# One kernel, two heads: exponential tables from integer phases and real magnitudes, and a new division of PSUM

## The chip, the cores and the metric

The kernel runs on one core of a Trainium2 chip. The metric is the device time of one execution in microseconds (us). The core has a matrix engine (TensorE, PE in the profile), a vector engine (VectorE, DVE), an activation engine (ScalarE, ACT), GpSimd (POOL) and SyncE (SP), whose queue issues nearly all of the transfers between HBM and the on-chip memory (SBUF). Matrix products land in PSUM, which has eight banks of 128 partitions x 512 words of four bytes.

## What is computed

Two heads of 512 columns each, for 2048 rows, are put side by side.

```
a = x @ dft_hid_re.T ; b = x @ dft_hid_im.T          # head A (FNet): x is 2048 x 512
yA = dft_seq_re @ a - dft_seq_im @ b                 # 2048 x 2048 matrices, given as inputs

dt = exp(log_dt)                                     # head B (S4D): 512 channels, 128 states
A  = -exp(log_A_real) + 1j * A_imag
C  = (C_real + 1j * C_imag) * dt[:, None]
P  = exp((A * dt[:, None])[:, :, None] * arange(2048))
K  = 2 * einsum("dn,dnl->dl", C, P).real             # a kernel of 2048 taps for each channel
yB = irfft(rfft(u, 4096) * rfft(K, 4096))[:2048] + u * D_skip
```

## The kernel before

**One order for all engines.** Nothing on the chip decides the order of the work. A planner in the program (class `Plan`) runs while the kernel is built: each step is a Python generator that yields the engine it wants and a duration that the planner books (`act(n)`, `dve(n)`, `load(kb)` or a constant for PE), and the step that can start first, by urgency among equals, is emitted next. Each engine then works through its list in that order and waits where an operand isn't there. Buffers and permits are `Sem` and `Ring` objects, completed values `Event` objects. An operation that takes longer on the chip than the planner booked does not change the order; it delays what stands behind it.

**Head A, class `Fnet`.** Four rows of a sequence matrix S that belong together (n, 1024 + n, 1024 - n, 2048 - n) agree up to their sign when S is a true DFT matrix. So of each four rows one (`base`) is multiplied in fp32 with the folded x, and the other three enter only by their deviations from it (`rest`, in bf16). `load_quad` loads one base tile and three `slots` tiles (128x512 fp32 each), computes the three deviations on DVE (L406, `same`, 52 instructions; L411, `own`, nine), writes a bf16 copy of the base (`rough`, L436, on ACT) and squares the deviations on ACT with a running sum (L439) for the guard. There are 32 such quads: four output blocks t, cosine and sine (c), four row blocks k. `sums` multiplies them with the folded x on PE: one fp32 product with the base (L493) and three bf16 products with the deviations (L496) for two column parts of 128, and for the cosine a third part of one column; then four bf16 products with `rough` for each half (L505). `outputs` multiplies the results with the hidden matrix (L558 in fp32, L559 in bf16), `evacuate` stores them. `loads` paces the quads: a group of four is let in every `GROUP_US` = 51 us, a quad every `QUAD_US` = 9 us. `guard` compares the sums of squares with thresholds; if S were not as assumed, `general` would recompute head A after the rest, under a branch.

**Head B, class `Ssm`.** The 2048 taps are split as l = 32 m + n: for each chunk of 32 channels (16 chunks) there are two complex tables, `t1` (32 entries for each channel, with C and dt in it) and `t2` (80 columns before), and PE multiplies them over the 128 states (`taps`, L1045, 64 products of 32 x 80). Both tables are built by repeated doubling. `seed_args` takes the parameters of the chunk, doubles the exponents up to 2^10 on ACT (L897), reduces the phases on DVE (L899 to L903) and takes Exp, Sin and Cos on ACT (L907 to L913); `seeds` multiplies them to complex seeds (L922). `tables1` and `tables2` then double the tables with complex products: `mul` (L852) makes four real products, `add` (L861) sums them. Even entries of `t2` are squares of earlier ones: ACT squares (L868), DVE subtracts (L881) and takes the doubled product (L875). The upper part of `t2` is in two forms, for which L1006 multiplies once more. `taps` is followed by the transform of the kernel along one axis (`stage1_k`, L1071), stored to HBM (`xk`, L1086). Meanwhile `spectrum_u` transforms u (L1125, evacuated by L1132, stored to `xu`). `spectra` reloads both in another order (L1180), `products` and `product` finish the transforms (L1208), multiply spectra (L1225, L1227) and start the inverse (L1241), stored to `zs` (L1253), reloaded (L1275) and finished by `inverse` (L1281, L1294, stored by L1288). The channels go through this in five units of 128, 128, 128, 64 and 64; a unit can start when its last chunk's tables are done.

**PSUM** is divided into four pairs of banks (`f0` to `f3`, permits `fs`), taken by `bank` and by `banks(2)`, which takes two pairs at once. The sums of head A hold one pair (sine) or two (cosine) for a whole group of four quads; `taps`, `stage1_k`, `stage1_u`, `product` and `inverse` take the others.

The last lines of the table step, which both the steps below and the prediction follow:

```
for j in range(4):
    p = yield from self.mul("prod", t, slice(0, 2 ** j), cs[:, :, 6 + j])
    yield from self.add(p, t, slice(2 ** j, 2 * 2 ** j))
```

## Time and profile before

| | |
|---|---|
| median of 2 runs | 529.36 us (529.35 to 529.37) |
| span of the profiled execution, first to last instruction | 527.8 us |
| what lies around the span (median less span; the execution's own time isn't listed apart) | 1.6 us |
| PE busy | 411.4 us, 78% of the span |
| DVE busy | 432.4 us, 82% |
| ACT busy | 362.1 us, 69% |
| moved by DMA | 113.59 MB, 215 GB/s on average |
| mean granted TensorE clock | 0.879 of full speed |

The profile is a page with the busy time of each engine, the span in 40 slices, the chain of work that ended last, and the costliest groups of instructions by line; the trace behind it can be asked for stretches of time, for single shapes and for a timeline. Durations are those of one execution. Matrix products are pipelined, so a busy PE need not be at its peak; where the granted clock is under 1, the same products take longer.

### The profile page before, as it was taken

What the parts mean: (1) busy time and instruction counts of PE and PEld (TensorE: products, weight loads), DVE (VectorE), ACT (ScalarE), POOL (GpSimd) and SP (SyncE); (2) the same over time, 40 slices, a digit from 0 to 9 for tenths busy, and PEclk for the clock granted to TensorE, in tenths of its full rate; (3) what the DMA queues carried; (4) which work ended last, traced back from release to release, by engine and by line L of the source; (5) the groups of instructions that cost most, each with busy time, mean ns of one, the idle gap of its engine ahead of it and who ended that gap; (6) DMA issues with size and microseconds to landing.
All of it is one profiled execution on the core that took longest, in us unless ns stands there. A gap on an engine that the chain in (4) does not pass through costs nothing.

```text
span 527.8 us, 13802 instructions
## 1 busy us (share of the span) xinstructions
PE 411.4 (78%) x5561; PEld 213.2 (40%) x5602; DVE 432.4 (82%) x763; ACT 362.1 (69%) x723; POOL 11.2 (2%) x21
## 2 busy tenths in 40 slices
PE   4589594559997988896999989967994999957421
PEld 3133121335453534353534444534541654646321
DVE  3999599998999899999999999999799999420300
ACT  1559699899699796759798979796587654433210
POOL 0000000000010000000010000003000000000000
PEclk7769886769999899999899999997796899975776
DMA  8989787866159937959959775719494156679851
GB/s 316 315 313 326 262 316 251 280 233 178 44 186 257 309 103 228 275 181 316 309 161 282 214 218 169 221 42 315 124 289 123 42 179 165 167 201 280 216 160 44
DMA packets 142532, 113.59 MB, mean 215 GB/s; under 512 B 68096, under 2 KB 112512, under 8 KB 142208
## 3 DMA queue, kind: packets, MB, share of 16 engines
q1 hardware_dynamic: 141744, 111.47, 68.6%
q10 hardware_dynamic: 720, 1.18, 0.6%
q8 instruction: 46, 0.75, 0.6%
q14 instruction: 22, 0.18, 0.1%
HBM read 78.09 MB, written 34.54 MB: 213 GB/s over the span
## 4 chain that ended last, share of the span: by engine, by line
DVE 36%; PE 30%; DMA 16%; ACT 6%; issue 5%; SPq 3%; POOL 1%; ACTq 0%; DVEq 0%; POOLq 0%
DVE prod L852 10%; PE f L558 6%; DVE t L861 6%; DMA slots<-in_sT 5%; PE f L1045 4%; DVE rest L406 4%; PE f L493 4%; PE f L1241 4%; PE f L1071 3%; DVE t L1006 3%; PE f L1281 3%; PE f L1208 2%; PE f L496 2%; DMA t<-zs 2%; DVE mid L1225 2%
## 5 line engine op out<-in xcount | busy, mean ns | idle before, releaser
L852 DVE TENSOR_TENSOR prod<-t,cs 128x1024 f32<-128x1024 f32 (+4 forms) x160 | 125.3, 797 | 1.9 <-ACT t L987 0.5
L861 DVE TENSOR_TENSOR t<-prod 128x512 f32<-128x512 f32 (+4 forms) x160 | 73.5, 475 | 0.9
L558 PE MATMUL f<-p,w 128*128 128x512 f32 x128 | 68.1, 614 | 6.0 <-ACT y L583 5.5
L406 DVE TENSOR_TENSOR rest<-slots,base 128x512 bf16<-128x512 f32 (+2 forms) x52 | 53.7, 1033 | 6.8 <-DMA slots<-in_sT 5.1
L1045 PE MATMUL f<-t,t 128*32 128x80 f32 x2048 | 45.1, 249 | 14.7 <-ACT big L1132 7.4
L439 ACT ACTIVATE slots<-rest 128x1536 f32<-128x1536 bf16 x32 | 47.3, 1479 | 12.3 <-DVE rest L406 8.6
L493 PE MATMUL f<-base,ec 128*128 128x512 f32 (+1 forms) x96 | 53.4, 639 | 0.0
L1045 PEld LDWEIGHTS f<-t,t 128*32 128x32 f32 x2048 | 40.9, 119 | 25.1 <-ACT big L1132 10.5
L493 PE MATMUL f<-base,es 128*128 128x512 f32 x64 | 38.2, 682 | 10.9 <-ACT xi L266 6.4
L496 PE MATMUL f<-rest,xr 128*128 128x512 bf16 (+1 forms) x134 | 38.8, 390 | 9.1 <-DVE rest L406 8.5
L868 ACT ACTIVATE square<-t 128x256 f32<-128x256 f32 (+1 forms) x64 | 36.3, 568 | 9.8 <-DVE t L881 5.8
L1006 DVE TENSOR_TENSOR t<-t,cs 128x1024 f32<-128x1024 f32 x32 | 38.9, 1217 | 0.0
L558 PEld LDWEIGHTS f<-p,w 128*128 128x128 f32 x128 | 22.5, 191 | 29.9 <-issue 18.6
L1208 PE MATMUL f<-big,w 64*32 64x256 f32 (+1 forms) x1024 | 30.4, 369 | 3.2 <-issue 2.6
L496 PEld LDWEIGHTS <-xr 128*128 128x128 bf16 (+1 forms) x144 | 13.7, 95 | 46.5 <-issue 40.9
L496 PE MATMUL f<-rest,xi 128*128 128x512 bf16 x86 | 27.3, 413 | 6.6 <-DVE rest L406 4.1
L1125 PE MATMUL f<-big,ib 64*128 64x512 f32 x64 | 20.8, 756 | 14.0 <-ACT big L1132 13.2
L1222 ACT ACTIVATE big<-f 128x1024 f32<-128x1024 f32 x28 | 27.4, 1019 | 5.0 <-PE f L1208 5.0
L881 DVE TENSOR_TENSOR t<-square 128x128 f32<-128x128 f32 (+1 forms) x64 | 24.7, 386 | 7.2 <-ACT square L868 7.2
L1071 PE MATMUL f<-ks,f1k 32*128 32x512 f32 (+1 forms) x192 | 22.0, 591 | 3.8 <-POOL ks L1060 3.6
L927 ACT ACTIVATE cs<-cs 128x352 f32<-128x352 f32 x32 | 15.6, 529 | 12.6 <-DVE cs L922 12.5
L1208 PEld LDWEIGHTS f<-big,w 64*32 64x32 f32 x1024 | 18.1, 108 | 14.0 <-issue 6.7
(147 smaller groups left out, 678.6 us busy)
## 6 DMA issues: line engine op xcount, KB each, us to landing
slots<-in_sT SPq DMA_DIRECT2D x93, 256.0 KB, 4.8
xu<-big SPq DMA_DIRECT2D x16, 512.0 KB, 4.5
base<-in_sT SPq DMA_DIRECT2D x31, 256.0 KB, 4.6
xk<-big SPq DMA_DIRECT2D x28, 256.0 KB, 3.4
big<-xu SPq DMA_DIRECT2D x24, 256.0 KB, 5.1
big<-xk SPq DMA_DIRECT2D x24, 256.0 KB, 5.6
zs<-mid SPq DMA_DIRECT2D x24, 256.0 KB, 2.8
big<-zs SPq DMA_DIRECT2D x12, 512.0 KB, 6.0
```

The costliest lines, as they stand in the source:

```text
L406: return v.tensor_tensor(rest[:, lo:hi:step], raw[:, lo:hi:step], base[:, None, :].to_broadcast([128, n, DM]), op=op)
L439: nc.scalar.activation(raw, rest, AF.Square, accum_out=self.stat[:, n:n + 1])
L493: nc.tensor.matmul(out, x[:, cols], base, start=k == 0, stop=False)
L496: nc.tensor.matmul(out, still[:, cols], rest[:, h], start=False, stop=k == 3 and h == 2)
L558: nc.tensor.matmul(ps, self.w[k][:, cols], self.p[t, c][:, d], start=k == 0, stop=False)
L852: self.nc.vector.tensor_tensor(p.rearrange("p k d c m -> p k (d c) m"), src.rearrange("p d c l -> p (d c) l")[:, None, :, rows].to_broadca ...
L861: self.nc.vector.tensor_tensor(dst[:, :, :, rows], p[:, 0], p[:, 1, :, ::-1], op=OP.add)
L868: self.nc.scalar.activation(sq, t[:, :, :, m // 2:m], AF.Square)
L1006: self.nc.vector.tensor_tensor(t[:, :, ::1 - 2 * k, 48 + 16 * k:64 + 16 * k], t[:, :, :, 1:32:2], cs[:, k, 5, :, :, None].to_broadcast([12 ...
L1045: nc.tensor.matmul(ps[32 * j:32 * j + 32, i], t1[:, d, c], t2[:, d, c], start=c == 0, stop=c == 1, tile_position=(0, 32 * j))
L1071: nc.tensor.matmul(out[:, :, 1] if a == 2 else out, self.f1k[r, min(a, 1)], taps, start=a == 0, stop=a == 2, tile_position=(32 * j, 0))
L1208: nc.tensor.matmul(both[:, :, c], self.w2[rows, R * q + r, xx, 32 * c:32 * c + 32], xs[rows, r, xx], start=True, stop=True, tile_position= ...
```

## The change

**Tables.** The complex doubling goes. For each chunk, two tables of phases (`phases1`, `phases2`) are grown by adding integers (a full turn is 2^32, wrapping), and two tables of real magnitudes (`magnitudes1`, `magnitudes2`) by real products; each has 5 or 6 DVE instructions. ACT turns each phase table into real and imaginary parts (`sines`: Abs, Sin, Sin), reading the phases across their layout, and one DVE product per table scales them by the magnitudes. `t2` has 64 columns instead of 80, of which 40 come this way and 24 are squares of earlier ones (`evens`, `squares`). Seeds are made for 64 channels at a time (`SET`), in eight sets; they hold exponents and phases instead of complex values. C enters as a magnitude and an angle, for which `params` computes a reciprocal, an Arctan and two sines, once for the first 64 channels and once for the other 448.

**Head A.** The bf16 copy `rough` goes: the low products read the upper halves of the fp32 base words (every second bf16). So the bases are held until the low products are done; there are 5 instead of 3. `same` becomes an instruction that also keeps the maximum of the deviations; ACT squares only the nine deviations of `own`. In exchange three products for each quad with a stationary column of ones sum the deviations over the partitions, and ACT squares that row once for each of the eight sums. `guard` has 14 small DVE instructions instead of eight.

**PSUM.** Three pairs, one bank `third` (the one-column part and the row of sums; one permit) and one bank `taps`. `stage1_k`, `stage1_u` and the first part of `products` take one pair at a time instead of two; the evacuations become steps of their own.

**Pace and constants.** `GROUP_US` 51 to 30, `QUAD_US` 9 to 6; urgencies of the table steps are new. The 32 inner positions of u are put in another order (`ORDER`) by the host's layout, as is one constant table.

```diff
-            return v.tensor_tensor(rest[:, lo:hi:step], raw[:, lo:hi:step],
-                                   base[:, None, :].to_broadcast([128, n, DM]), op=op)
+            col, self.tops = self.tops, self.tops + 1
+            return v.tensor_tensor_reduce(rest[:, lo:hi:step], raw[:, lo:hi:step],
+                                          base[:, None, :].to_broadcast([128, n, DM]), 1.0, 0.0, op, OP.max,
+                                          self.stat[:, col:col + 1])
...
-        nc.scalar.activation(rough, base, AF.Copy)
...
-        nc.scalar.activation(raw, rest, AF.Square, accum_out=self.stat[:, n:n + 1])
+        for h, n, col in squares:
+            yield "act", act(512 * n) + 0.1
+            nc.scalar.activation(raw[:, h:h + n], rest[:, h:h + n], AF.Square, accum_out=self.stat[:, col:col + 1])
...
+            yield "pe", 0.2 if not c else 0.66, None, 6
+            for h in range(3):
+                nc.tensor.matmul(third[32:33], self.ones, rest[:, h], start=k == 0 and h == 0, stop=k == 3 and h == 2,
+                                 tile_position=(0, 32))
+            self.plan.put(self.rests)
...
-                nc.tensor.matmul(low[:, d], self.xb[t, c, k][:, 128 * d:128 * d + 128], self.m[t, c, k][2], start=k == 0,
-                                 stop=k == 3)
+                nc.tensor.matmul(low[:, d], self.xb[t, c, k][:, 128 * d:128 * d + 128],
+                                 self.m[t, c, k][0].bitcast(BF16)[:, 1::2], start=k == 0, stop=k == 3)
...
-        self.slots, self.fs, self.one = [0, 1, 2, 3], Sem(4), Sem(1)
+        self.slots, self.fs, self.one, self.tapss = [0, 1, 2], Sem(3), Sem(1), Sem(1)
...
+    rises = (5, 4, 1, 1), (6, 4, 2, 2), (8, 4, 4, 3), (12, 4, 8, 4), (3, 1, 1, 4), (20, 0, 20, 5)
...
+    def grow(self, p, seed, to, of, m):
...
+        yield "dve", dve(m * CHUNK)
+        self.nc.vector.tensor_tensor(p[:, to:to + m], p[:, of:of + m],
+                                     seed[:, None, :].to_broadcast([128, m, CHUNK]), op=OP.add)
...
+            for j in range(5):
+                yield from self.grow(p, s[:, 6 + j], 2 ** j, 0, 2 ** j)
...
+    def sines(self, re, im, p, sign):
...
+        a, n = self.nc.scalar, math.prod(re.shape[1:])
+        yield "act", act(n) + 0.15
+        a.activation(re, p, AF.Abs)
+        yield "act", act(n) + 0.15
+        a.activation(im, p, AF.Sin, scale=sign * TWO_PI / TURN)
+        yield "act", act(n) + 0.15
+        a.activation(re, re, AF.Sin, scale=-TWO_PI / TURN, bias=self.halfpi)
...
+    def sines2(self, n):
+        yield self.t2s
+        t, p = self.t2[n % 2], self.p2.rearrange("p (h l) d -> p d h l", h=2)
+        yield from self.sines(t[:, :, :, 0, :20], t[:, :, :, 1, :20], p, 1.0)
...
+        yield from self.sines(t[:, :, 0], t[:, :, 1], self.p1.rearrange("p m d -> p d m"), -1.0)
...
+    def scale(self, p, seed, to, of, m):
...
+        yield "dve", dve(m * CHUNK)
+        self.nc.vector.tensor_tensor(p[:, :, to:to + m], p[:, :, of:of + m],
+                                     seed[:, :, None].to_broadcast([128, CHUNK, m]), op=OP.mult)
...
+            yield "dve", dve(80 * CHUNK)
+            v.tensor_tensor(t, t, p.rearrange("p d (h l) -> p (d h) l", h=2)[:, :, None, :].to_broadcast(
+                [128, 2 * CHUNK, 2, 20]), op=OP.mult)
...
+            yield "dve", dve(64 * CHUNK)
+            v.tensor_tensor(t, t, p[:, :, None, :].to_broadcast([128, CHUNK, 2, 32]), op=OP.mult)
...
+        yield from self.squares(t[:, :, 0, :, 4:20], t[:, :, :, :, 20:28])
+        yield from self.squares(t[:, :, 0, :, 20:28], t[:, :, :, :, 28:])
...
-BASES, SLOTS, RESTS, STAGED, ROUNDS = 3, 2, 2, 2, 6
-GROUP_US, QUAD_US, AHEAD_US = 51.0, 9.0, 20.0
+BASES, SLOTS, RESTS, STAGED = 5, 2, 2, 2
+GROUP_US, QUAD_US, AHEAD_US = 30.0, 6.0, 20.0
```

More of the change, by code (lines that the diff above doesn't have):

```diff
@@ new lines, in load_tables @@
+        self.p1, self.p2 = (tab.tile([128, m, CHUNK], I32, name=f"phase{m}") for m in (32, 40))
+        self.square = tab.tile([128, 16 * CHUNK], F32, name="square")
+        self.mag = tab.tile([128, 72 * CHUNK], F32, name="mag")
+        self.both = [tab.tile([128, 2, 12, SET], F32, name=f"seeds{m}") for m in range(2)]
+        self.par = tab.tile([128, 4, SET], F32, name="par")
+        second = self.t2[1].rearrange("p d h c l -> p (d h c l)")
+        n = DM - SET
+        self.rest = second[:, :4 * n].rearrange("p (a d) -> p a d", a=4)
@@ L818, in setup_rest @@
         yield self.dt_ev
-        yield from self.params(par, par[:, 0], dt)
-        self.plan.put(self.t1s)
-        yield self.pars
-        self.par[1] = self.tab.tile([128, 4, CHUNK], F32, name="par", bufs=2)
-        yield "act", act(4 * CHUNK)
-        self.nc.scalar.activation(self.par[1], par[:, :, :CHUNK], AF.Copy)
-        self.plan.set(self.par1_ev)
+        yield from self.params(par, par[:, 0], dt, self.angle_tmp2)
+        for _ in range(2):
+            self.plan.put(self.t1s)
         yield "dma", load(900)
```

693 lines of the change are left out of this document (373 added, 320 removed).

## The prediction

> **What bounds the kernel now.** I read the page first: the busy times and the slices of the span.
>
> ```profile
> span 527.8 us, 13802 instructions
> PE 411.4 (78%) x5561; PEld 213.2 (40%) x5602; DVE 432.4 (82%) x763; ACT 362.1 (69%) x723; POOL 11.2 (2%) x21
> ...
> DVE  3999599998999899999999999999799999420300
> ```
>
> DVE is nearly full from the second slice to the 34th, then almost idle. So I cut the span where DVE's last table operation ends, at 449 us by the timeline below, and asked for busy time by stretch (columns: length, busy time and count of PE, its weight loads, DVE, ACT and POOL; then the granted TensorE clock, the DMA share and GB/s).
>
> ```profile
> core 0: us, PE busy (x) PEld busy (x) DVE busy (x) ACT busy (x) POOL busy (x), PEclk, DMA share, GB/s
> 20.00:100.00 80.00, 55.80 (x241) 19.66 (x246) 72.72 (x139) 61.92 (x130) 0.00 (x0) 0.77 0.85 298
> 100.00:450.00 350.00, 304.00 (x4123) 154.48 (x4154) 335.10 (x588) 272.54 (x543) 10.16 (x7) 0.94 0.65 198
> 450.00:528.00 78.00, 41.44 (x1177) 33.31 (x1176) 13.03 (x20) 20.57 (x32) 0.23 (x1) 0.75 0.69 181
> ```
>
> From 20 to 450 us, the main stretch, DVE works 72.7 + 335.1 = 407.8 of 430 us, 95%; PE 359.8 (84%) and ACT 334.5 (78%). The last 78 us are another kernel: DVE has 13 us of work, and the last unit of channels goes through its chain of small steps. The timeline and the chain of waits show the seam and one loss in the tail:
>
> ```profile
> 448.63 0.69 DVE L861 TENSOR_TENSOR t<-prod 128x512 f32<-128x512 f32 x1
> 450.07 2.42 PE L1045 MATMUL f<-t,t 128*32 128x80 f32 x128
> 460.09 2.06 ACT L1078 ACTIVATE t<-f 128x512 f32<-128x512 f32 x4 [1.33 <-PE f L1071]
> 470.15 2.37 SPq L1086 DMA_DIRECT2D xk<-t  x4
> ```
>
> The last taps start 0.8 us after DVE's last table operation: the end is set by when the tables are done, plus a tail. In the tail the last store of `xk` had its data at 462.15 us and was issued at 470.15, behind other transfers in SP's queue. The span is 1.6 us short of the median of 529.36; I add that back at the end.
>
> **DVE, the tables.** What goes is nine groups, L852 to L903 (below L852, L861 and the last; L1006, L881, L875, L922, L899 and L901 lie between):
>
> ```profile
> L852 DVE TENSOR_TENSOR prod<-t,cs 128x1024 f32<-128x1024 f32 (+4 forms) x160 | 125.3, 797 | 1.9 <-ACT t L987 0.5
> L861 DVE TENSOR_TENSOR t<-prod 128x512 f32<-128x512 f32 (+4 forms) x160 | 73.5, 475 | 0.9
> L903 DVE TENSOR_SCALAR seed<-seed 128x352 f32<-128x352 f32 x16 | 5.3, 334 | 0.0
> ```
>
> Their sum is 317.9 us. For what comes I use a price per instruction of 0.155 us plus 1.037 ns per column, from the shapes with 1024 and 32 columns:
>
> ```profile
> L1006 DVE TENSOR_TENSOR t<-t,cs 128x1024 f32<-128x1024 f32 x32 | 38.9, 1217 | 0.0
> L793 DVE SCALAR_TENSOR_TENSOR par<-par,cs 128x32 f32<-128x32 f32 x1 | 0.2, 186 | 0.0
> ```
>
> A chunk now has 22 growing steps (2 x 36 x 32 and 2 x 31 x 32 columns, 4288), two scalings (2560 + 2048) and six operations for the even entries (1536): 30 instructions, 10432 columns, 4.65 + 10.82 = 15.5 us, times 16 is 247.5. Each of the eight seed sets reduces 704 phases: two scalar operations at half the column price (L903: 352 columns in 334 ns) and two full ones, 1.7 us, 13.7 in all. Integer operands appear in no row; I take them at the fp32 price, because they are as wide. Half of it, as for L903, would take 18 us more off, and double would add 36. So 317.9 go and 261 come: -57 us. `params` grows from 4 to 25 instructions for each of its two blocks: 17 at the full and six at half the column price and one of double length are 14 us for 448 columns and 5 for 64. The reciprocal, which no row shows, is put between half and twice the full price, 0.3 to 1.2 us: about 20 against 3.4 now (eight instructions at the same price), +17. Guard: six more tiny operations, +1.
>
> **DVE, the deviations.** 52 instructions of `same` keep a maximum as well. No row shows such an instruction. Nearest are the two-input operation with one more step, at the same 512 columns, and what ACT pays for reading its accumulator out:
>
> ```profile
> L406 DVE TENSOR_TENSOR rest<-slots,base 128x512 bf16<-128x512 f32 x25 | 17.1, 683 | 0.0
> L411 DVE SCALAR_TENSOR_TENSOR rest<-base,small,slots 128x512 bf16<-128x512 f32 x8 | 6.0, 744 | 0.0
> L439 ACT ACTIVATION_READ_ACCUMULATOR slots<-rest 128x1 f32 x32 | 6.1, 189 | 0.0
> ```
>
> 744 - 683 = 61 ns or 189 ns each: 3 to 10 us, a gain is excluded since the old work stays in it; I take 6. DVE in all: -57 + 17 + 1 + 6 = -33 us, 375 of work in the main stretch.
>
> **ACT.** Fifteen groups of the tables go, 179.8 us together, the largest L868, the smallest L895; 31 of the 32 loads of a function table (L907, L909) are among them, at 1.283 us each.
>
> ```profile
> L868 ACT ACTIVATE square<-t 128x256 f32<-128x256 f32 (+1 forms) x64 | 36.3, 568 | 9.8 <-DVE t L881 5.8 <-DVE t L861 4.0
> L909 ACT ACT_TABLE_LOAD x16 | 20.5, 1283 | 0.3
> L907 ACT ACT_TABLE_LOAD x15 | 19.2, 1283 | 0.2
> L907 ACT ACTIVATE seed<-seed 128x352 f32<-128x352 f32 x16 | 7.9, 496 | 0.2
> L913 ACT ACTIVATE seed<-seed,halfpi 128x352 f32<-128x352 f32 x16 | 9.2, 577 | 0.0
> L895 ACT ACTIVATE seed<-par 128x64 f32<-128x64 f32 x16 | 4.0, 253 | 2.1 <-DMA par<-par_dram 2.1
> L439 ACT ACTIVATE slots<-rest 128x1536 f32<-128x1536 bf16 x32 | 47.3, 1479 | 12.3 <-DVE rest L406 8.6 <-DVE rest L411 2.5 <-issue 1.1
> L436 ACT ACTIVATE rough<-base 128x512 bf16<-128x512 f32 x32 | 19.8, 620 | 0.0
> ```
>
> From 64 and 1536 columns (253 and 1479 ns) an ACT instruction costs 0.2 us plus 0.833 ns per column, and 0.08 more with a bias tile (L913 against L907). Per chunk: three of 1280 (3.9), three of 1024 (3.2), four squares (2.1), small copies (1.5), taps of 512 (0.6): 11.3, times 16 is 181. Per seed set nine instructions with 2240 columns, 3.7, plus two table loads, 2.6, times 8 is 50. So the tables cost 231 against 180: +51. In head A L436 (19.8), L439 with its read-outs (53.4) go, nine smaller squares (8) and eight rows of sums (6) come: -59. Arctan and sines of `params`, with three or four table loads, +7. That is -1, before one open price: four of the six large instructions of a chunk read their phases in steps of 32 words, 4608 columns.
>
> ```profile
> L967 ACT ACTIVATE t<-par 128x64 f32<-128x64 f32 x16 | 4.9, 305 | 0.0
> L852 DVE TENSOR_TENSOR prod<-t,cs 128x128 f32<-128x128 f32 x32 | 11.7, 373 | 0.6 <-ACT t L987 0.5
> L861 DVE TENSOR_TENSOR t<-prod 128x128 f32<-128x128 f32 x16 | 4.6, 289 | 0.1
> L1078 ACT ACTIVATE big<-f 128x512 f32<-128x512 f32 x28 | 14.7, 594 | 7.6 <-PE f L1071 7.6
> L1247 ACT ACTIVATE mid<-f 128x512 f32<-128x512 f32 x28 | 15.2, 591 | 10.6 <-PE f L1241 10.6
> ```
>
> Scattered words have a price in two rows: L967 writes every word 64 words from the last, 305 against L895's 253 ns, 0.8 ns per word; L852 with one entry reads scattered words on DVE, 373 against L861's 289 ns, 0.66 per word; their mean is 0.73. L1078, which reads PSUM across its layout on ACT, pays nothing against L1247. The new case shares the engine and the side with the last and the memory with the others, so I take half of 0.73, 0.36 ns: 4608 x 16 x 0.36 = +27 us, with 0 and +54 as the ends. [...] ACT in the main stretch: 334.5 - 1 + 27 = 360 us.
>
> **PE.** Taps shrink from 80 to 64 columns, `stage1_k` from 12 products to eight. 96 products with the ones come.
>
> ```profile
> 143.20 0.86 PE f L493 x2
> 144.71 0.86 PE f L493 x2
> 146.22 2.35 PE f L1045 x128
> L496 PE MATMUL f<-rest,xr 128*1 128x512 bf16 x48 | 13.0, 379 | 0.0
> ```
>
> One fp32 and three bf16 products take 1.51 us there, of which 0.86 the first: 0.22 us each for the others. So the ones cost 96 x 0.22 = 21 us, 36 by the row of the one-column products, and down to nothing where they run beside the cosine's one-column part; I take 16. Taps save up to a fifth of 2.35, 0.45 x 16 = 7, `stage1_k` 3. The low products' second-of-two reading shows in no row; 64 products at nothing to 0.22 more, 0 to 14; I take 0 because the words stay in order. PE: +6, 366 us in the main stretch.
>
> **Pace, buffers, tail.** The quads' loads move forward on SP's queue by up to 147 us (from 51 to 30 us a group); they pass the stores and reloads of `xu` and `xk`. I cost that at nothing: after 100 us the DMA share is 0.65. Uncovered it costs what DVE waits for late slots now, 5.1 us in L406's row below, for each time that it doubles. Bases are held to the end of their group, so a load of the next group can wait in SP's queue for the low products, and stores and reloads of `xu`, `xk` and `zs` stand behind it; the price of one such block is the 8 us of L1086. `sums` waits for the one `third` bank: behind it stands the rest of PE's list while ACT evacuates two halves and squares a row, 3 x 0.6 us, seven times, 13 us of PE at most; products of head B between two halves hide it, and I take nothing. `ORDER` changes constants alone. With head A's products done earlier PE has more room when the last tables come. The tail keeps its steps; SP's order in it is new, and the 8 us above can vanish or double, so I leave it.
>
> **The sum.** In the main stretch DVE has 375, PE 366, ACT 360 us. Three engines so even will not repeat 95%: there is one buffer for the phases of each table, so DVE's next phases wait until ACT has read the last, and its scalings wait for ACT's sines. At 92.5% the stretch is 375 / 0.925 = 405, 25 less than 430: 527.8 - 25 + 1.6 = **504 us**. DVE at 95% gives 494, at 90% 516: that is this case's own range.
>
> **Rivals.**
> ACT takes over. At the full 0.73 ns ACT has 387 us, more than DVE. At 92.5% that is 418, 517 us; at 90% 430, 529. For it speak L967 and L852; against it L1078. It decides from 0.56 ns per word on, where ACT's work passes DVE's 375.
> PE and PSUM take over. With 36 us for the ones and 14 for the low products PE has 360 + 36 + 14 - 10 = 400, and three pairs instead of four can make it wait longer for evacuations; at 93% 430, no gain: 525 to 535. For it: PE's 84% now; against: the granted clock was 0.77 from 20 to 100 us, so a denser PE could be a faster one.
> Slower: the instruction that keeps the maximum streams at half rate. L406 takes 53.7 us for its 52 now (25 of 683 ns, the rest longer); doubled, DVE has 375 + 48 = 423 us, at 95% 445, 15 more than now, and PE waits for the deviations as well: 545 to 550. It decides from about 0.75 us extra each, where DVE is back at 408. [...]
> The change doesn't do what it says: if integer sums did not wrap or the guard fired, head A would be run again by `general`; no row prices that, and I give it a chance within the remainder.
>
> ```profile
> L406 DVE TENSOR_TENSOR rest<-slots,base 128x512 bf16<-128x512 f32 (+2 forms) x52 | 53.7, 1033 | 6.8 <-DMA slots<-in_sT 5.1 <-ACT square L868 0.9 <-issue 0.8
> ```
>
> **How the numbers follow.** Forecast 0.50, ACT 0.20, PE and PSUM 0.12, half rate 0.10; 0.08 are left for a shorter tail or free scattered reads below 494 and for failures above. About 2% (519 and 540) is what a measurement of this kernel can tell from no change. Faster: all of the forecast, half of ACT's, little of PE's, half the remainder: 0.65. Slower: half rate, a sliver of PE's and the remainder: 0.12. Within 2%: 0.23. The range goes from 486, DVE at 95% with a tail 8 us shorter, to 531, which takes in ACT's and most of PE's case.
>
> **What would show it.** DVE's busy time near 400 us, `same` at 683 + 60 to 190 ns, the phases' Abs and Sin between 1.27 and 2.2 us for 1280 columns (which decides between forecast and first rival), about 20 table loads, ones products at 0.2 to 0.4 us, the last taps near 425 us and some 78 us after them. I am wrong if DVE's density in the main stretch falls below 88% with every price as taken: then the order itself, or three pairs, holds the kernel.

## The result and the profile after

The changed kernel takes 607.6 us (607.5 to 607.69), against 529.36 before: a ratio of 1.148, 95% interval 1.1445 to 1.1512. The forecast was 504 us in a range of 486 to 531. Here and in the table below, times are medians of a kernel's fast runs: one run of `twos_four_pairs` and two of `head_order`, each more than 1.5% above the fastest of its kernel, are left out. The page of the changed kernel, with its busy times and two of its rows of 40 slices:

```profile
span 605.8 us, 13828 instructions
PE 430.5 (71%) x5602; PEld 208.0 (34%) x5634; DVE 391.3 (65%) x843; ACT 424.0 (70%) x662; POOL 10.9 (2%) x25
```
```profile
DVE  4996988656696757969976566589694563233110
ACT  2247488999979698886699697789948973434420
```

DVE has 41 us less to do than before, as meant. But the row of nines is gone: no engine is now full anywhere for long. The last taps show where the span splits (the first row ends with the start of the first and of the last of their 2048 products), and the busy times by stretch (columns as in the prediction) what each part holds:

```profile
L1151 PE MATMUL taps<-t,t x2048: 216/219/317, 103.7 to 507.9; 128*32 128x64 f32 x187
```
```profile
20.00:100.00 80.00, 49.62 (x160) 15.50 (x161) 70.72 (x161) 48.13 (x91) 0.29 (x1) 0.83 0.78 267
100.00:505.00 405.00, 307.10 (x3790) 141.81 (x3817) 289.05 (x633) 339.50 (x510) 9.30 (x7) 0.89 0.53 161
505.00:605.80 100.80, 62.96 (x1624) 44.73 (x1625) 20.32 (x31) 31.94 (x48) 0.23 (x1) 0.82 0.78 203
```

Both parts grew. The main stretch is 485 us, 55 more, with DVE busy 70.7 + 289.1 = 359.8 us of it: 74%, where it was 95%. ACT has 387.6 (80%), PE 356.7 (74%). The last product of the taps starts at 507.9 us, and 97.9 us follow, against 75.5 before (452.3 to 527.8, from the same view). The groups by shape of the sines, and the two scalings of the tables that wait for them:

```profile
L1022 ACT ACTIVATE t<-phase 128x1280 f32<-128x1280 int32 x16 | 39.5, 2466 | 10.2 <-DVE phase L977 5.8 <-PE taps L1151 4.4
L1024 ACT ACTIVATE t<-phase 128x1280 f32<-128x1280 int32 x16 | 38.8, 2424 | 0.1
L1022 ACT ACTIVATE t<-phase 128x1024 f32<-128x1024 int32 x16 | 31.9, 1995 | 1.6 <-DVE phase L977 1.6
L1024 ACT ACTIVATE t<-phase 128x1024 f32<-128x1024 int32 x16 | 31.7, 1981 | 0.0
L1026 ACT ACTIVATE t<-t,halfpi 128x1280 f32<-128x1280 f32 x16 | 21.6, 1351 | 0.0
```
```profile
L1067 DVE TENSOR_TENSOR t<-t,mag 128x2560 f32<-128x2560 f32 x16 | 45.2, 2824 | 36.8 <-ACT t L1026 36.8
L1088 DVE TENSOR_TENSOR t<-t,mag 128x2048 f32<-128x2048 f32 x16 | 36.6, 2290 | 49.7 <-ACT t L1026 49.7
```

The four large instructions that read phases in steps of 32 words take nearly twice the time of L1026, which reads words in a row: 2.4 against 1.35 us for 1280 columns. And DVE stands for 36.8 + 49.7 = 86.5 us in front of L1067 and L1088 until the last sine is done. PE stands too (its waits, in us, with the count and the longest):

```profile
PE f L1238 <- ACT big L1247: 34.9, 6, 14.9
PE taps L1151 <- DVE t L1088: 24.4, 6, 9.6
PE f L587 <- ACT y L612: 18.7, 8, 4.1
```

L1247 and L612 only carry finished products out of PSUM. They are late although they take 1013 and 589 ns each: something else is ahead of them on ACT. The longest of these waits shows what. PE's product ends at 85.1 us; ACT then runs six large instructions of the sines in a row, nine small operations after them, and only then the evacuation (start and length in us; first and last of the sines, the evacuation, and PE's next product):

```profile
85.95 2.41 ACT L1022 ACTIVATE t<-phase 128x1280 f32<-128x1280 int32 x1 [0.57 <-DVE phase L977]
95.59 1.13 ACT L1026 ACTIVATE t<-t,halfpi 128x1024 f32<-128x1024 f32 x1
98.93 1.00 ACT L1247 ACTIVATE big<-f 128x1024 f32<-128x1024 f32 x1
```
```profile
99.98 3.79 PE L1238 MATMUL f<-big,ib 64*128 64x512 f32 x8 [14.87 <-ACT big L1247]
```

### The profile page after: what moved, and what is told of

It is laid out like the page before. It is cut to its first block, busy times and chain, and to the rows that moved or that the text cites. A ratio compares the mean times of both kernels' runs of the same rounds, so it can differ in the third digit from the quotient of the medians.

```text
span 605.8 us, 13828 instructions
## 1 busy us (share of the span) xinstructions
PE 430.5 (71%) x5602; PEld 208.0 (34%) x5634; DVE 391.3 (65%) x843; ACT 424.0 (70%) x662; POOL 10.9 (2%) x25
## 5 line engine op out<-in xcount | busy, mean ns | idle before, releaser
L587 PE MATMUL f<-p,w 128*128 128x512 f32 x128 | 73.8, 661 | 19.8 <-ACT y L612 18.7
L1022 ACT ACTIVATE t<-phase 128x1280 f32<-128x1280 int32 (+1 forms) x32 | 71.2, 2230 | 11.8 <-DVE phase L977 7.4
L1024 ACT ACTIVATE t<-phase 128x1280 f32<-128x1280 int32 (+1 forms) x32 | 70.5, 2203 | 0.1
L1067 DVE TENSOR_TENSOR t<-t,mag 128x2560 f32<-128x2560 f32 x16 | 45.2, 2824 | 36.8 <-ACT t L1026 36.8
L1088 DVE TENSOR_TENSOR t<-t,mag 128x2048 f32<-128x2048 f32 x16 | 36.6, 2290 | 49.7 <-ACT t L1026 49.7
L1046 DVE TENSOR_TENSOR mag<-mag,seeds 128x32 f32<-128x32 f32 (+5 forms) x176 | 61.9, 361 | 2.9 <-ACT mag L1059 2.4
L1151 PE MATMUL taps<-t,t 128*32 128x64 f32 x2048 | 38.4, 242 | 25.5 <-DVE t L1088 24.4
L977 DVE CUSTOM_DVE_ANT_0 phase<-seeds,phase 128x512 uint16<-128x512 uint16 (+4 forms) x128 | 52.8, 417 | 0.5
L1151 PEld LDWEIGHTS taps<-t,t 128*32 128x32 f32 x2048 | 35.6, 125 | 35.6 <-DVE t L1088 13.3
L416 DVE CUSTOM_DVE_ANT_1 rest<-slots,base 128x1024 bf16<-128x1024 f32 (+1 forms) x27 | 36.7, 1358 | 4.6 <-PE third L520 2.4
L1026 ACT ACTIVATE t<-t,halfpi 128x1280 f32<-128x1280 f32 (+1 forms) x32 | 39.6, 1247 | 0.0
L514 PE MATMUL f<-base,ec 128*128 128x512 f32 x64 | 35.9, 643 | 0.6 <-ACT low L567 0.6
L1319 PE MATMUL f<-big,w 64*32 64x256 f32 (+1 forms) x768 | 25.8, 392 | 14.4 <-ACT p L548 5.7
L520 PE MATMUL third<-rest,small 128*1 128x512 bf16 x96 | 26.4, 384 | 0.0
```

The costliest lines, as they stand in the source:

```text
L416: return v.tensor_tensor_reduce(rest[:, lo:hi:step], raw[:, lo:hi:step], base[:, None, :].to_broadcast([128, n, DM]), 1.0, 0.0, op, OP.max ...
L514: nc.tensor.matmul(out, x[:, cols], base, start=k == 0, stop=False)
L587: nc.tensor.matmul(ps, self.w[k][:, cols], self.p[t, c][:, d], start=k == 0, stop=False)
L977: self.nc.vector.tensor_tensor(p[:, to:to + m], p[:, of:of + m], seed[:, None, :].to_broadcast([128, m, CHUNK]), op=OP.add)
L1022: a.activation(re, p, AF.Abs)
L1024: a.activation(im, p, AF.Sin, scale=sign * TWO_PI / TURN)
```

## The experiments

The theories: **A**, the scattered reads lengthen ACT's work, and DVE waits for it in its fixed order. **B and D**, the three pairs of PSUM banks (and the ones products) hold PE; in `contig`, B takes in the written order too. **C**, the written order does not suit the new work. **E**, the pace of head A. **F**, the tables' part loses whatever the order. **G**, the planner's wrong booking of the sines. **H**, one urgency. "Last taps" in the table is the start of the last product of the taps, and "tail" the span from there on, both from the same view as above. They are those of the profiled run, which can be 5 us from the median (538.9 us in `contig`).

| run | what differs | us | ratio to before, 95% | last taps | tail |
|---|---|---|---|---|---|
| before | | 529.4 | | 452.3 | 75.5 |
| after | the change | 607.6 | 1.1445 to 1.1512 | 507.9 | 97.9 |
| contig | reads in a row | 544.1 | 1.0238 to 1.0387 | 439.4 | 97.6 |
| in_twos | phases in twos | 549.1 | 1.0291 to 1.0448 | 450.5 | 97.8 |
| tables_only | without head A's part | 628.8 | 1.1829 to 1.2019 | 506.6 | 120.2 |
| head_only | head A's part alone | 512.5 | 0.9636 to 0.9774 | 437.7 | 72.4 |
| twos_four_pairs | in_twos, four pairs | 563.9 | 1.0571 to 1.0717 | 435.1 | 129.2 |
| twos_pace | in_twos, pace 51 and 9 us | 555.8 | 1.0479 to 1.0567 | 429.8 | 126.8 |
| twos_tables_only | in_twos without head A's part | 573.1 | 1.0755 to 1.09 | 451.0 | 121.9 |
| twos_order | in_twos, new constants | 513.4 | 0.9692 to 0.978 | 431.6 | 78.7 |
| scattered_booked | after, true bookings | 611.6 | 1.1511 to 1.1649 | 503.8 | 108.8 |
| scattered_order | the same, new constants | 547.6 | 1.0293 to 1.0425 | 470.6 | 75.2 |
| twos_four_order | in_twos, four pairs, new constants | 504.6 | 0.9527 to 0.9635 | 423.6 | 78.6 |
| head_order | head_only, new constants | 516.4 | none (two runs, 513.0 and 519.7 us) | 444.0 | 73.8 |
| twos_tables_order | twos_tables_only, new constants | 539.1 | 1.014 to 1.029 | 455.8 | 81.1 |
| no_ones | twos_four_order without the ones | 503.3 | 0.9482 to 0.9591 | 422.0 | 77.7 |
| sines_first | twos_order, sines' urgency back | 557.3 | 1.0493 to 1.0597 | 437.2 | 117.9 |
| sines_first_four | twos_four_order, the same | 544.2 | 1.0237 to 1.0339 | 425.8 | 117.7 |
| pace_back_four | twos_four_order, pace back | 506.2 | 0.9537 to 0.9638 | 426.4 | 78.1 |

### The price of the scattered reads: contig and in_twos

`contig` reads the phases in the order in which they lie; `in_twos` keeps the right phases but stores two neighbouring entries of a channel side by side.

```diff
-        t, p = self.t2[n % 2], self.p2.rearrange("p (h l) d -> p d h l", h=2)
+        t = self.t2[n % 2]
+        p = self.p2.rearrange("p m d -> p (m d)").rearrange("p (d h l) -> p d h l", h=2, l=20)
```

> The changed kernel, but Abs and the first Sin of each chunk read the phases in the order in which they lie, one word after the other; the same 64 instructions with the same columns in the same order, so the tables hold the phases of other entries (the right assignment of phases to entries is left out). Theory A, the scattered reads and the DVE that stands in its fixed order behind the late sines: the 1280-column Abs falls from 2.47 to about 1.35 us, the 1024-column one from 2.0 to 1.14, ACT's work by about 62 us, DVE's idle time at L1067 and L1088 from 86 to under 30 us, and the time to 535 to 550 us. Theory B, the written order or the three pairs of PSUM banks: the price falls as well, but the time stays above 590 us because the waits move elsewhere.

```diff
-        self.p1, self.p2 = (tab.tile([128, m, CHUNK], I32, ...) for m in (32, 40))
+        self.p1, self.p2 = (tab.tile([128, m // 2, CHUNK, 2], I32, ...) for m in (32, 40))
+    def double(self, s, *js):
+        for j in js:
+            self.nc.gpsimd.tensor_copy(self.twice[j]..., s[:, j, :, None].to_broadcast([128, CHUNK, 2]))
...
+        v.tensor_tensor(p[:, to // 2:(to + m) // 2], p[:, of // 2:(of + m) // 2],
+                        self.twice[seed][:, None, :].to_broadcast([128, m // 2, 2 * CHUNK]), op=OP.add)
```

> The changed kernel with each table's phases stored in twos (two neighbouring entries of one channel lie side by side), so that Abs and the first Sin read runs of two words; the result is the same, 128 small GpSimd copies double the seeds. If the price is one per separate run, the extra 0.9 ns per word halves: 1280 columns in about 1.9 us and, by theory A, 565 to 585 us in all. If words that share an aligned eight bytes cost nothing extra, 1.35 us and the time of the contiguous run. Theory B: above 590 us in both cases.

The groups of `contig` (the sines, then the scalings), and behind them those of `in_twos`:

```profile
L1022 ACT ACTIVATE t<-phase 128x1280 f32<-128x1280 int32 x16 | 20.3, 1267 | 10.7 <-DVE phase L977 5.7 <-PE taps L1151 4.9
L1024 ACT ACTIVATE t<-phase 128x1280 f32<-128x1280 int32 x16 | 20.1, 1259 | 0.1
L1022 ACT ACTIVATE t<-phase 128x1024 f32<-128x1024 int32 x16 | 16.7, 1044 | 2.0 <-DVE phase L977 2.0
L1024 ACT ACTIVATE t<-phase 128x1024 f32<-128x1024 int32 x16 | 16.7, 1043 | 0.0
```
```profile
L1067 DVE TENSOR_TENSOR t<-t,mag 128x2560 f32<-128x2560 f32 x16 | 45.2, 2824 | 12.2 <-ACT t L1026 11.8
L1088 DVE TENSOR_TENSOR t<-t,mag 128x2048 f32<-128x2048 f32 x16 | 36.6, 2289 | 19.4 <-ACT t L1026 19.3
```
```profile
L1034 ACT ACTIVATE t<-phase 128x1280 f32<-128x1280 int32 x16 | 21.5, 1341 | 10.8 <-DVE phase L986 5.8 <-PE taps L1165 4.9
L1081 DVE TENSOR_TENSOR t<-t,mag 128x2560 f32<-128x2560 f32 x16 | 45.2, 2825 | 12.5 <-ACT t L1038 12.5
L1102 DVE TENSOR_TENSOR t<-t,mag 128x2048 f32<-128x2048 f32 x16 | 36.6, 2290 | 19.8 <-ACT t L1038 19.6
```

Per chunk the four instructions of the changed kernel take 1199 + 1165 + 951 + 938 = 4253 ns more than in `contig`, for 4608 words: 0.92 ns per scattered word, 68 us in all. In twos almost all of that is gone (74 ns more than in a row, 0.06 ns per word), and DVE's waits at the scalings fall from 86.5 to 32 us in both runs (under 30 were expected). Theory A holds, at 58.5 us of the time in this written order (607.6 against the 549.1 of `in_twos`). It is not the whole of it: with nearly free reads the kernel is still 3 to 4% slower than before, the last taps come earlier than before (439 and 451 us), and the tail keeps its 98 us.

### The two parts of the change: tables_only, head_only, twos_tables_only

`tables_only` and `head_only` each take class `Fnet` and its constants from one kernel and all the rest from the other, with four pairs of banks. In `tables_only` a buffer of u is loaded again before its product is issued, so part of head B's output is that of other rows.

```diff
-        yield self.tapss
-        ps = self.fps.tile([128, 8, 2, 32], F32, name="taps")
+        k, pair = yield from self.bank()
+        ps = pair[:, 0].rearrange("p (i h l) -> p i h l", h=2, l=32)
...
-class Fnet: (after)
+class Fnet: (before; in head_only the other way round)
```

> Only the tables' part of the change: head A is that of the kernel before (rounded copies of S, squares of all three deviations, no maxima, no ones products, 51 and 9 us a group and a quad), PSUM is four pairs, the taps take half a pair. Theory A: the loss is in the tables, so the time is at or above the changed kernel's, 600 to 640 us, with the same 80 us or more of DVE waits on the sines. Theory B (PSUM, ones and pace): 525 to 550 us.

> Only head A's part of the change, on the tables of the kernel before: no rounded copies, maxima in `same`, the ones products (their row lies in a pair, for PSUM is four pairs), bases held to the end of a group, 51 and 9 us. ACT loses about 59 us of work, PE gains 20 to 40. Theory A: no loss here, 505 to 530 us. Theory B: this part, or its holding of bases and its ones products, costs most of the 78 us: above 560 us.

> Only the tables' part of the change, with phases in twos; head A, the four pairs and the pace are those of the kernel before, the result is right. Theory F, the tables' part loses by itself even at contiguous prices, because ACT has 50 us more work and DVE, PE and ACT wait for each other within each chunk: 550 to 580 us. Theories C to E alone, in which the tables' 57 us less of DVE's work come through: 500 to 530 us. (In the earlier run with the tables alone a buffer of u was loaded again before its product was issued, so part of head B's output came from other rows; here the two buffers have a semaphore each.)

All of the loss is on the tables' side (628.8 us; 573.1 with phases in twos), and head A's part alone is a gain of 17 us. How that gain comes about, the stretches of `head_only` show, and DVE's largest wait, first in the kernel before (20 to 450 us), then in `head_only` (100 to 440 us):

```profile
20.00:100.00 80.00, 58.77 (x304) 22.02 (x305) 78.63 (x160) 53.71 (x123) 0.00 (x0) 0.86 0.83 296
100.00:437.00 337.00, 299.24 (x4214) 148.16 (x4214) 329.50 (x609) 227.17 (x481) 4.17 (x7) 0.95 0.67 204
```
```profile
DVE t L881 <- ACT square L868: 7.2, 7, 3.8
```
```profile
DVE prod L878 <- ACT t L1013: 1.1, 1, 1.1
```

DVE's tables are the old ones, but now it works 408.1 of 417 us, 98%: ACT, with 281 us of work instead of 334, is hardly ever late. Before, DVE's waits for ACT came to 11.7 us from 20 to 450 us, and 5.1 us more were waits for head A's slots; in `head_only`, to 440 us, 3.4 us and none are left, and the last taps are 14.6 us earlier. So work taken off an engine that was not the bound paid, because the bound waited for it. Head A's part also holds its bases longer and brings its own order of the work; what of the gain is theirs, no run separates.

### Is it PSUM, or the pace: twos_four_pairs, twos_pace

```diff
-        self.slots, self.fs, self.one, self.tapss = [0, 1, 2], Sem(3), Sem(1), Sem(1)
+        self.slots, self.fs, self.one = [0, 1, 2, 3], Sem(4), Sem(1)
-        third = self.ssm.fps.tile([128, 512], F32, name="third")
+        self.third_bank, pair = yield from self.ssm.bank()
+        third = pair[:, 0]
```
```diff
-GROUP_US, QUAD_US, AHEAD_US = 30.0, 6.0, 20.0
+GROUP_US, QUAD_US, AHEAD_US = 51.0, 9.0, 20.0
```

From here on the kernels with the new tables give each of the two buffers of u a semaphore of its own; no run has that alone.

> The kernel with phases in twos and PSUM as four pairs again: the taps take half a pair, a group's third row takes half a pair and holds it to the end of the group; nothing else of the work changes. Theory D (three pairs hold PE): 515 to 535 us. Theory C: no gain, 540 to 565 us, since a pair taken for the third row gives back what the fourth pair brings.

> The kernel with phases in twos and the pace of before, 51 and 9 us instead of 30 and 6. Theory E, the pace: head A's quads, moved forward, push the products of head B into the tail; back at 51 us the tail shrinks by the 20 us and the time is 520 to 535 us. Theories C and D: within 10 us of 549.

Both are slower than `in_twos`, by 15 and 7 us: in this order neither the pairs nor the pace is what holds the kernel, and theories D and E fall as the main cause. In both the last taps come early (435 and 430 us), and the loss is in a tail of 127 to 129 us. One of PE's groups in the tail of `twos_pace`, from 429.8 us on:

```profile
L587 PE MATMUL f<-p,w 128*128 128x512 f32 x32 | 17.9, 643 | 1.1 <-ACT y L612 0.7 <-issue 0.2
```

A last group of head A's outputs is left over there, and products of its sums too; in the kernel before they had been done by then. That points at the written order, without showing it: the tables come in time, the other work does not.

### The order: twos_order, scattered_booked, scattered_order, head_order

Of the steps that could start at the same time, the planner starts the one with the lowest urgency. Its constants were chosen anew for the same instructions:

```diff
-SEEDS, SINES, EVENS, FIRST1, FIRST2 = 1.5, -0.5, 1.9, 2.0, 1.9
+SEEDS, SINES, EVENS, FIRST1, FIRST2 = -2.91, 2.84, -2.01, 3.37, 1.97
-GROUP_US, QUAD_US, AHEAD_US = 30.0, 6.0, 20.0
+GROUP_US, QUAD_US, AHEAD_US = 30.0, 10.8, 20.0
```

> The kernel with phases in twos, the same instructions on each engine, with five constants of the planner changed (urgencies of seeds, sines, even entries and first tables, and 10.8 instead of 6 us from quad to quad), so that only the written order differs. Theory C, the written order: with the scattered reads gone, what is left of the loss (549 us instead of the forecast 504) is DVE standing in its fixed order behind the sines (31 us) and products of unit 2 written into the tail (20 us); a better order gives 505 to 530 us. Theory D, three pairs and the ones: no order of the same work helps by more than 8 us: 540 us or above.

For the scattered reads first the booking alone, then also the constants (-0.91, 3.49, 2.14, 2.6, 1.9, `UNIT` 0.0 instead of 0.05, and a pace of 61.0, 8.1, 20.9):

```diff
-        yield "act", act(n) + 0.15
+        yield "act", 0.25 + 1.75e-3 * n
         a.activation(re, p, AF.Abs)
-        yield "act", act(n) + 0.15
+        yield "act", 0.25 + 1.75e-3 * n
         a.activation(im, p, AF.Sin, scale=sign * TWO_PI / TURN)
```

> The changed kernel with its scattered reads, but the planner books Abs and the first Sin at what the trace shows (2.49 us for 1280 columns, 2.04 for 1024, instead of 1.33 and 1.11) and writes its order by that; urgencies unchanged. Theory G, the wrong booking is what makes DVE stand: DVE's idle time at L1067 and L1088 falls from 86 to under 40 us and the time to 560 to 580 us. Theory C, the urgencies do not suit the work, whatever is booked: 590 to 620 us.

> The same with scattered reads booked at their true length, and the planner's urgencies and pace chosen anew for it. The instructions are those of the changed kernel. Theory C in its full form, the order alone lost the time and ACT's 424 us of work could be hidden: 505 to 530 us. Theory A in its full form, the 62 us of ACT cannot be hidden by any order: 565 us or above. Between them, 535 to 560 us: both count, and the reads cost what is above the 513 us that the order reached with phases in twos.

In `head_order` the constants of the old tables are new:

```diff
-FIRST_TABLE, T1, SEEDS = 0.01, 0.005, 1.5
-UNIT, EARLY = 0.05, 4
+FIRST_TABLE, T1, SEEDS = 0.786, 0.32, -1.63
+UNIT, EARLY = 0.02, 6
-GROUP_US, QUAD_US, AHEAD_US = 51.0, 9.0, 20.0
+GROUP_US, QUAD_US, AHEAD_US = 53.8, 12.5, 8.5
```

> Head A's part of the change on the tables of before (512.5 us with the old constants), with urgencies and pace chosen anew. There DVE worked 410 of the 420 us up to 440, so an order has little left to give: 500 to 515 us. If the gain of the new order in twos was only that any order can be bettered by 7%, this one falls below 495 us.

The order is worth 36 us in twos and 60 with the scattered reads. Booking the reads at their true length without touching the urgencies is worth nothing (611.6), so theory G falls. On the old tables the one other set of constants that was run gave no gain (513.0 and 519.7 us against 512.5, where 500 to 515 were expected), which speaks against the notion that any order can be bettered. The reads still cost 34 us between kernels with constants of their own (547.6 and 513.4), against 58.5 with those of the change: each cause makes the other dearer. The stretches of `twos_order`, split near the last taps:

```profile
20.00:100.00 80.00, 62.45 (x188) 20.16 (x190) 70.58 (x156) 48.87 (x99) 8.16 (x17) 0.87 0.86 300
100.00:431.00 331.00, 290.84 (x4072) 138.28 (x4105) 297.92 (x643) 284.78 (x527) 52.60 (x119) 0.97 0.67 200
431.00:510.30 79.30, 45.08 (x1325) 32.66 (x1313) 16.84 (x25) 25.88 (x39) 0.47 (x1) 0.82 0.82 210
```

PE now works 353.3 of 411 us (86%) and DVE 368.5 (90%), and the tail is back at 79 us.

### Which constant: sines_first, sines_first_four, pace_back_four

```diff
-SEEDS, SINES, EVENS, FIRST1, FIRST2 = -2.91, 2.84, -2.01, 3.37, 1.97
+SEEDS, SINES, EVENS, FIRST1, FIRST2 = -2.91, -0.5, -2.01, 3.37, 1.97
```

> The kernel with phases in twos and a new order (513.4 us), with one constant back: the sines' urgency at -0.5, ahead of everything else on ACT, instead of 2.84. Theory H, the urgency is what spoiled the order, since sines written ahead hold up the evacuations of PSUM that PE waits for: 535 to 555 us, as with all old constants (549), and PE's waits for evacuations (L587, L1252) rise from 10 to over 25 us. If it takes all the constants together: 510 to 525 us.

> The kernel with phases in twos, four pairs and a new order (504.6 us), again with the sines' urgency alone back at -0.5, from 3.35. Theory H: 530 to 555 us. If it takes all the constants together: 502 to 515 us.

> The kernel with phases in twos, four pairs and a new order (504.6 us), with the pace alone back at 30, 6 and 20 us from 41.6, 13.1 and 7.8. Theory H: the pace decides little, 503 to 515 us. If the pace was the point: 530 us or above.

The sines' urgency alone costs 44 us with three pairs (557.3 us, 2 above the range of theory H) and 40 with four; the pace costs 2, no more than the runs scatter. Most of the 44 and 40 is not in the tables: the last taps are only 5.6 and 2.2 us later, but the tails are 118 us instead of 79. PE's group of the transform of u in `sines_first`, then in `twos_order`, shows the way there:

```profile
L1252 PE MATMUL f<-big,ib 64*128 64x512 f32 x64 | 20.0, 708 | 30.9 <-ACT big L1261 28.3 <-ACT low L567 1.5 <-ACT p L548 0.9
```
```profile
L1252 PE MATMUL f<-big,ib 64*128 64x512 f32 x64 | 19.0, 684 | 5.0 <-ACT low L567 1.5 <-ACT big L1261 1.4 <-ACT p L548 1.3
```

L1261 is an evacuation of PSUM, the successor of L1247 above. With the sines ahead on ACT, PE waits 28.3 us for it instead of 1.4, and longer at the taps too; the same wait in `sines_first` and in `twos_order`:

```profile
PE taps L1165 <- DVE t L1102: 22.6, 5, 9.9
```
```profile
PE taps L1165 <- DVE t L1102: 7.5, 6, 2.2
```

The two differences, 27 and 15 us, are nearly the 44. What PE does not get done beside the tables is done behind them, in the chain of small steps: from the last taps on, PE has 82.6 us of work in `sines_first` (below) and 45.1 in `twos_order` (its last stretch above):

```profile
437.20:555.10 117.90, 82.64 (x1861) 53.77 (x1851) 26.25 (x39) 42.20 (x62) 0.23 (x1) 0.86 0.88 234
```

Theory H holds: this urgency is enough to lose the time. With four pairs the waits are spread over more lines, and the time says the same. The step the other way, the changed kernel or `in_twos` with this one constant new, was not run, so whether it is enough to win the time back stays open.

### What is left: twos_four_order, twos_tables_order, no_ones

`twos_four_order` has four pairs, phases in twos, the constants 2.52, 3.35, 3.1, 2.0, 1.9 (and `UNIT, EARLY` 0.0, 5) and a pace of 41.6, 13.1 and 7.8 us.

> Phases in twos, four pairs in PSUM, urgencies and pace chosen anew for that. If the fourth pair is worth something once the order fits, 495 to 508 us; if PSUM never mattered, 510 to 520 us, as the three pairs with a new order (513.4).

It is the fastest kernel found, 504.6 us, 4 to 5% below the kernel before. Its stretches up to the last taps:

```profile
20.00:100.00 80.00, 55.98 (x225) 18.59 (x231) 76.67 (x175) 49.68 (x99) 8.85 (x17) 0.83 0.82 288
100.00:423.00 323.00, 292.44 (x4053) 140.41 (x4081) 290.75 (x624) 281.54 (x527) 84.05 (x119) 0.97 0.71 212
```

DVE works 367.4 of 403 us, 91%. Going to four pairs went with 9 us less here and 15 more in the old order; its constants differ from those of `twos_order`, so the 9 us cannot be given to the pair alone.

`twos_tables_order` is `twos_tables_only` with the constants 0.67, 1.64, 2.0, 3.72, 3.35, `UNIT, EARLY` 0.0, 6, and a pace of 51.0, 9.0, 24.0.

> The tables' part alone with phases in twos (573 us with the old constants), with urgencies chosen anew for it. Theory F, the tables' part loses by itself even where reads are cheap, because ACT has 50 us more work and head A's old squares and copies on top (414 us in all): 530 us or above. Theory C, it lost by the order alone, and its 40 us less of DVE's work come through in part: 505 to 525 us.

In an order of its own the tables' part alone still loses 1.4 to 2.9% (539.1 us), and the whole change in twos with four pairs is 34 us faster than that. The busy times on the pages of `twos_tables_only` and `head_only`:

```profile
PE 417.7 (73%) x5502; PEld 205.6 (36%) x5538; DVE 395.2 (69%) x785; ACT 414.2 (72%) x740; POOL 79.7 (14%) x151
```
```profile
PE 424.7 (83%) x5698; PEld 209.3 (41%) x5698; DVE 434.6 (85%) x821; ACT 312.1 (61%) x661; POOL 5.7 (1%) x23
```

The tables alone bring ACT from 362.1 to 414.2 us, and head A's part alone takes 50 us from it: the one needs the room that the other makes. In that sense theory F holds. That this is why the two together gain more than head A's part alone (504.6 against 512.5 us) is argued from these sums, not shown by a run.

```diff
-            for h in range(3):
-                nc.tensor.matmul(third[32:33], self.ones, rest[:, h], ..., tile_position=(0, 32))
...
-        self.nc.scalar.activation(row, row, AF.Square, accum_out=self.stat[32:33, n:n + 1])
```

> The kernel with phases in twos, four pairs and a new order (504.6 us), without the 96 products with the ones and the squares of their rows; the order of all other instructions is unchanged (the check of the sums of the deviations is left out). PE has 26 us less to do. If PE sets the pace where the ones stand, 485 to 495 us; if they fill waits, 500 to 506 us.

The group of the ones in the changed kernel:

```profile
L520 PE MATMUL third<-rest,small 128*1 128x512 bf16 x96 | 26.4, 384 | 0.0
```

Without these 26.4 us of PE's work the time is 503.3 instead of 504.6, a difference that the runs cannot tell from none: in this order the ones fill waits.

## Why the prediction was wrong

**The work was counted well.** DVE was to have 432.4 - 33 = 399 us; it has 391.3. Sums of integers cost what fp32 costs, as assumed (817 and 816 ns, in the last section). `same` takes 683 ns for 512 columns as before and reading the maximum 81, 4.2 us in all where 6 were taken. ACT without the open price was to have 361 us; `contig` has 357.7:

```profile
PE 414.5 (77%) x5634; PEld 200.9 (37%) x5634; DVE 390.2 (73%) x843; ACT 357.7 (67%) x662; POOL 11.3 (2%) x25
```

PE was to gain 6 us and gained 19 (430.5); ten of the 13 more are the ones, 26.4 us where 16 were taken, within the bounds of 0 and 36; in the order of `no_ones` this size did not matter.

**The first step that failed: "so I take half of 0.73, 0.36 ns".** It is 0.92 ns per word, 68 us instead of 27 and beyond the upper end of 54. The two rows that priced scattered words in SBUF (0.66 and 0.8) were the right kind, if still too low; the row that reads PSUM (594 against 591 ns), for whose sake the price was halved, was not.

**The second: "At 92.5% the stretch is 375 / 0.925 = 405".** The density is 74% in the changed kernel, and with reads in a row, every price as taken (that of the reads at its lower end, nothing), 86%, by the stretches of `contig`: 73.6 + 285.6 = 359.2 of 419 us.

```profile
20.00:100.00 80.00, 54.22 (x220) 17.61 (x223) 73.60 (x168) 47.25 (x99) 0.29 (x1) 0.83 0.79 275
100.00:439.00 339.00, 289.90 (x3869) 134.73 (x3861) 285.55 (x627) 274.04 (x502) 9.69 (x7) 0.96 0.63 190
```

That is below the 88% at which the prediction called itself wrong, "then the order itself, or three pairs, holds the kernel". It was the order: with phases in twos, still three pairs, and new constants DVE is back at 90% (`twos_order`). The 92.5% were carried over from the 95% of a kernel in which DVE's waits came to 17.6 us from 20 to 450 us. The prediction did name the new waits, DVE for ACT's sines, and gave them 2.5 points, some 11 us of the stretch; in front of the two scalings they are 86.5 us, and 31.6 with reads in a row. In the new tables DVE waits twice in each chunk for three instructions of ACT, and these were written ahead of PSUM's evacuations. The urgency behind this, `SINES = -0.5`, is in the changed kernel; the prediction priced what the sines take and never asked what stands behind them on ACT. Where the order fits (`twos_four_order`) DVE has 367 us in a stretch of 403, 91%, so a density near the forecast's can be had with these tables. That its time, 504.6 us, is the forecast's 504 is in part luck: its reads in twos cost next to nothing (0.06 ns more per word, measured in `in_twos`) and it has four pairs. With scattered reads and three pairs, as in the change, the fastest order that was run takes 547.6 us.

**The third: "The tail keeps its steps".** From the last taps on 97.9 us are left instead of 75.5, and 97.6 with reads in a row. PE's products of the spectra in the tail before (L1208, from 452.3 us on) and after (L1319, from 507.9 us on):

```profile
L1208 PE MATMUL f<-t,w 64*32 64x128 f32 x256 | 5.1, 309 | 1.6 <-issue 1.6
L1208 PE MATMUL f<-big,w 64*32 64x128 f32 x256 | 4.4, 273 | 0.0
```
```profile
L1319 PE MATMUL f<-t,w 64*32 64x128 f32 (+1 forms) x512 | 11.5, 315 | 1.6 <-issue 1.4 <-ACT big L1335 0.3
L1319 PE MATMUL f<-big,w 64*32 64x128 f32 (+1 forms) x192 | 4.3, 308 | 0.1
```

704 are left where 512 were, and in all PE has 63.0 us of work in the last stretch instead of 41.4. No term of the sum could see that work not done beside the tables comes back behind them.

**The rivals.** "ACT takes over" was nearest in its mechanism and short in its time: with the measured 68 us ACT has 334.5 - 1 + 68 = 401.5 us, at 92.5% a stretch of 434 and 533 us in all, 75 below the measurement, since it shared the forecast's density and tail. "PE and PSUM take over" falls as the main cause with `twos_four_pairs`, where a fourth pair gains nothing, and with `twos_order`, where three pairs reach 513.4 us; some of the 9 us from there to `twos_four_order` may be the pair's. The instruction at half rate did not occur, and no run shows such a rate: with the maximum it takes 683 ns for 512 columns, as the plain one did, and 81 ns to read the maximum out. The quads moved forward were costed at nothing and cost next to nothing: 506.2 us with the change's 30 and 6 us (`pace_back_four`) against 504.6 with 41.6 and 13.1, and in `twos_pace` the pace of the kernel before was 7 us slower, not faster. That the change would not do what it says did not occur either.

## What to carry to other kernels

A share of busy time belongs to an order, not to an engine: before it is carried over to changed work, look for each moved step at what it will wait for and at what is queued behind it on its new engine, evacuations of PSUM above all. Work taken off an engine with slack pays where the bound waits for that engine (17 us in `head_only`), and work put there can cost for the same reason (DVE's 86.5 us in front of the scalings of the changed kernel). Where ACT reads a table across its rows, let neighbouring words be read in pairs (58.5 us in `in_twos`).

## What the runs showed of the hardware

ACT reads single words 32 words apart at 0.92 ns per word more than words in a row (2466 against 1267 ns for 1280), and pairs of neighbouring words, 64 words apart, at 0.06 ns more (1341 ns). Pairs from an odd word on were not tried.

The instruction that keeps a maximum is no slower than the one without: with two fp32 sources of 512 columns it takes 683 ns, as the plain one did (L406 before). A second one of 81 ns reads the maximum out. The rows of both in the changed kernel:

```profile
L416 DVE CUSTOM_DVE_ANT_0 rest<-slots,base 128x512 bf16<-128x512 f32 x25 | 17.1, 683 | 0.0
L416 DVE DVE_READ_ACCUMULATOR2_ANT small<- 128x1 f32 x52 | 4.2, 81 | 0.0
```

A sum of 32-bit integers shows in the trace as halves of 16 bits, twice the columns, and takes the time of an fp32 product of as many words:

```profile
L977 DVE CUSTOM_DVE_ANT_0 phase<-seeds,phase 128x1280 uint16<-128x1280 uint16 x16 | 13.1, 817 | 0.1
L1046 DVE TENSOR_TENSOR mag<-mag,seeds 128x640 f32<-128x640 f32 x16 | 13.1, 816 | 0.0
```
